# Load order, slot order, whole tail tiles, low parts on GpSimd: five small edits to a fused three-stage kernel

## The chip, the cores and the metric

The kernel runs on one core of a Trainium2 chip. The metric is the device time of one execution in microseconds, median over runs. One execution was also recorded by the hardware profiler; its times are from that one execution, and it has a time of its own.

TensorE multiplies matrices into PSUM, VectorE (DVE), ScalarE (ACT) and GpSimd (POOL) work element by element, and SyncE (SP) issues most of the transfers.

## The reference, cut to what matters

Three modules follow each other, for 8 batches of 576 tokens and 512 features (8 heads of 64).

```
# 1 retention
ret  = (q @ k.T / 8) * (gamma[h] ** (i - j) where i >= j else 0)   # B=8 H=8 S=576 D=64
x    = (ret @ v) with the heads side by side                       # [B, 576, 512]
# 2 attention by experts: 4 experts, the best 2 by gate
logits = x @ w_gate;  w = softmax of the best 2
for e in 4 experts:
    q, k, v = x @ wq[e], x @ wk[e], x @ wv[e]                      # 64 wide
    out += w[e] * (causal_softmax(q @ k.T / 8) @ v) @ wo[e]
# 3 mixing, with x = out
theta = x @ w_theta
y = w_tok_r @ (x * cos(theta)) + w_tok_i @ (x * sin(theta))        # over the tokens
u = x + y
return u + relu(u @ w_ch)
```

## The kernel before, in words

**Exact products.** An fp32 product is made of two rounded parts. `split` (L102) writes the high part with ACT and the low part, source minus high part, with VectorE. `mm3` (L97) is three matmuls: high by high, high by low and low by high. Nearly every matrix of stages 2 and 3 thus has a high and a low tile (`WH`, `WL`; `xh`, `xl`; `zh`, `zl`; `uh`, `ul`).

**Tiling.** The 576 tokens are five tiles of 128, 128, 128, 128 and 64 rows (`ROWS`). The tail, the tile of 64, is in places joined with the tail of the other batch of a pair: tile 4 of a pair g holds rows 0 to 63 of the first batch's tail and rows 64 to 127 of the second's.

**Stage 1** is a recurrence over the tiles. `ret_scores` (L136) makes the scores of a tile in two PSUM tiles called `w` and multiplies them by the decay; `ret_out` (L157 to L178) updates the state, makes the output in another `w` tile, and turns it into `xt`, `xh` and `xl`: VectorE (L175), ACT (L177), GpSimd (L178). `proj_qk` (L198 to L215) makes queries and keys of a half of the tokens (288 wide): twelve matmuls into one `w` tile, then its split. A key (`KN`) takes one ACT and one VectorE instruction, a query (`U`) two of each. `proj_v` (L229) makes the values and the gate's logits of one tile: four matmuls with the high part of x and of the weights, four with the low part of the weights, four with the low part of x.

**The weights** of the projections, `w1`, are 4 tiles of 128 x 772: columns 0 to 511 belong to queries and keys, 512 to 771 to values and gate. `load_w1` (L400) loads one tile whole, `split_w1` (L405) splits it. At the start (L486 to L502) the first batch's five retention steps, its value projections and its first query and key are written out by hand, with `work(-1, ...)` naming the projections.

**Stage 2** runs 80 slots (b, p, m), ten for each batch: scores of a query tile, softmax, transposes, products. Beside it each slot does what the table `SLOTS` (L43) names: projections ("Q01" the queries of expert pair 0 and token half 1, "K" keys, "v2" the values of tile 2, "g" the gate; small letters are of the next batch), and a retention step of the next batch (R0 to R5). `LAST` is the table of the last batch. The PSUM pool that holds `w` has three buffers (`WB`), used in turn by projections, scores of retention and its output. A job list turns the fp64 weights of stage 3 into high and low parts (`convert`, L421 to L441, mostly VectorE, ACT and GpSimd): 40 jobs for theta and token weights, due up to slot `JOBS[0]`, and 13 for the channel weights, due up to `JOBS[1]`.

**Stage 3**: `token_tile` makes x and theta of a tile, `z_tile` (L551) makes x cos and x sin and splits them (`zh`, `zl`; the tail's `zth`, `ztl`). `mix` (L656) adds in four PSUM accumulators the token products (L693), and x by a transpose on TensorE (`add_x`, L683), for one batch and one half of the features: 16 times. Then u is split, and `channel` (L706) multiplies it by the channel weights, GpSimd adding the low part at the end (L719). The gate's products for the outputs of stage 2 (`load_o`, L514) stand on GpSimd.

**What sets the order.** Up to the end of stage 2 TensorE runs its instructions in the order of the program. The other engines' order, and TensorE's in stage 3, is set by a scheduler when the kernel is built; each engine then runs its list in order.

## Time and profile before

| | |
|---|---|
| median of 3 runs | 955.18 us (954.91 to 955.77) |
| the profiled execution | 958.07 us, span 956.3 us |
| TensorE matmuls | 925.0 us, 97% of the span |
| TensorE weight loads | 854.3 us, 89% |
| VectorE | 643.0 us, 67% |
| ScalarE | 441.0 us, 46% |
| GpSimd | 247.8 us, 26% |

Busy times are sums over the span, and overlap. A busy share of 97% is a mean: stages with waits stand beside stages without. TensorE's granted clock is a share of full speed; at full speed it runs at 2.4 GHz, at half at 1.2 GHz. Stages 1 and 2 take the time up to about 514 us, with a passage to 541 us; the mixing takes the rest.

### The profile page before, as it was taken

The page shows a single profiled execution, that of the slowest core. Times are in us where ns is not written, and L with a number is a line of the kernel's source. Part 1 is how long each engine was busy: PE and PEld are TensorE (multiplying, and loading weights), DVE is VectorE, ACT ScalarE, POOL GpSimd, SP SyncE. Part 2 cuts the span into 40 slices and gives each one's busy share as a digit, 9 for nine tenths or more (in the row PEclk, how much of TensorE's full clock was granted, in tenths as well). Part 3 has the DMA queues.
Part 4 walks back from the last instruction along what each step waited for, and adds up shares of the span by engine and source line. Part 5 has one row for each costly group of instructions (what it writes and reads, how often), then busy time and mean ns, then how long its engine had stood idle before and what let it go on. Part 6 is the DMA issues. An engine that isn't in the chain of part 4 may idle for free.

```text
span 956.3 us, 21524 instructions
## 1 busy us (share of the span) xinstructions
PE 925.0 (97%) x8090; PEld 854.3 (89%) x8090; DVE 643.0 (67%) x1843; ACT 441.0 (46%) x1198; POOL 247.8 (26%) x290
## 2 busy tenths in 40 slices
PE   6989999999999999999999799999999999999998
PEld 5879989898998989988778799999999999999998
DVE  5377777867688787777669845684648755485623
ACT  2255555655565665555666414343234532344320
POOL 6315243452434434242312120111202101020100
PEclk9999999999999999999999899999999999999999
DMA  9757666576665666645784210111101001010001
GB/s 273 204 143 209 177 201 161 165 229 182 201 171 175 197 196 202 166 124 155 214 304 156 98 51 1 63 38 51 51 1 50 26 12 39 1 51 1 25 26 50
DMA packets 81016, 115.69 MB, mean 121 GB/s; under 512 B 17680, under 2 KB 55952, under 8 KB 80912
## 3 DMA queue, kind: packets, MB, share of 16 engines
q1 hardware_dynamic: 80768, 114.03, 40.1%
q8 instruction: 64, 1.05, 0.5%
q0 software_dynamic: 144, 0.28, 0.2%
q14 instruction: 40, 0.33, 0.1%
HBM read 71.94 MB, written 23.74 MB: 100 GB/s over the span
## 4 chain that ended last, share of the span: by engine, by line
PE 79%; DVE 9%; ACT 5%; DMA 3%; issue 2%; SPq 1%; POOL 1%; DVEq 0%; ACTq 0%; POOLq 0%
PE acc L693 24%; PE w L98 8%; PE w L99 8%; PE w L100 8%; PE w L229 6%; PE a L294 5%; PE w L136 5%; PE a L360 4%; PE a L341 3%; PE w L164 3%; PE w L168 3%; PE acc L683 2%; ACT P L302 2%; PE pS L157 1%; DVE U L215 1%
## 5 line engine op out<-in xcount | busy, mean ns | idle before, releaser
L693 PE MATMUL acc<-TK,zh 128*128 128x256 f32 (+1 forms) x1024 | 185.9, 304 | 3.7 <-DVE ul L104 2.4
L693 PEld LDWEIGHTS acc<-TK,zh 128*128 128x128 f32 x1024 | 154.1, 192 | 4.3 <-issue 2.6
L302 ACT ACTIVATE P<-P,st 128x128 f32<-128x128 f32 (+4 forms) x160 | 95.7, 599 | 76.1 <-DVE st L297 75.3
L693 PE MATMUL acc<-TK,zl 128*128 128x256 f32 (+1 forms) x512 | 111.1, 298 | 0.0
L719 POOL TENSOR_TENSOR o<-o,ul 128x576 f32<-128x576 f32 x28 | 42.4, 1519 | 222.3 <-DVE o L714 214.1
L693 PEld LDWEIGHTS acc<-TK,zl 128*128 128x128 f32 x512 | 87.1, 191 | 0.1
L561 ACT ACTIVATE cs<-cs 128x512 f32<-128x512 f32 x72 | 45.2, 630 | 90.7 <-DVE cs L559 85.0
L297 DVE CUSTOM_DVE_ANT_0 P<-a,cm 128x128 f32<-128x128 f32 (+4 forms) x160 | 72.1, 477 | 14.8 <-PE a L294 14.2
L98 PE MATMUL w<-uh,CH 128*128 128x256 f32 (+1 forms) x256 | 76.0, 298 | 3.3 <-ACT uh L103 2.6
L563 DVE SCALAR_TENSOR_TENSOR cs<-cs,x 128x512 f32<-128x512 f32 x72 | 62.0, 868 | 25.0 <-ACT cs L561 24.8
L294 PE MATMUL a<-KK,U 128*64 128x288 f32 (+4 forms) x384 | 76.8, 328 | 2.0 <-issue 0.9
L103 ACT ACTIVATE zh<-cs 128x512 fp32r<-128x512 f32 x64 | 40.3, 630 | 81.7 <-PE acc L693 65.3
L104 DVE TENSOR_TENSOR zl<-cs,zh 128x512 fp32r<-128x512 f32 x64 | 44.6, 699 | 48.9 <-ACT zh L103 48.1
L98 PE MATMUL w<-xh,WH 128*128 128x288 f32 x256 | 76.0, 297 | 0.0
L99 PE MATMUL w<-ul,CH 128*128 128x256 f32 (+1 forms) x256 | 75.7, 296 | 0.0
L100 PE MATMUL w<-uh,CH 128*128 128x256 f32 (+1 forms) x256 | 75.7, 296 | 0.0
L100 PE MATMUL w<-xh,WL 128*128 128x288 f32 x256 | 75.3, 294 | 0.0
L99 PE MATMUL w<-xl,WH 128*128 128x288 f32 x256 | 75.3, 294 | 0.0
L136 PE MATMUL w<-qz,kt 128*64 128x128 f32 (+1 forms) x576 | 57.5, 323 | 9.8 <-DVE U L215 7.3
L437 POOL TENSOR_TENSOR r<-r,ex 128x192 f32<-128x192 f32 (+1 forms) x51 | 29.5, 579 | 142.0 <-ACT hl L438 59.0
L104 DVE TENSOR_TENSOR ul<-acc,uh 128x256 fp32r<-128x256 f32 x64 | 25.8, 451 | 59.2 <-ACT uh L103 58.8
L294 PEld LDWEIGHTS a<-KK,U 128*128 128x128 f32 (+1 forms) x384 | 53.6, 171 | 12.6 <-issue 6.2
(141 smaller groups left out, 2265.9 us busy)
## 6 DMA issues: line engine op xcount, KB each, us to landing
kv<-kv SPq DMA_DIRECT2D x40, 512.0 KB
KK<-KN SPq DMA_DIRECT2D x128, 144.0 KB
raw<-wd SPq DMA_DIRECT2D x43, 192.0 KB
qz<-qk SPq DMA_DIRECT2D x64, 128.0 KB
kt<-qk SPq DMA_DIRECT2D x32, 256.0 KB
out<-o SPq DMA_DIRECT2D x28, 288.0 KB
td<-hl SPq DMA_DIRECT2D x27, 192.0 KB
TK<-td SPq DMA_DIRECT2D x9, 576.0 KB
```

The source lines that it names most:

```text
L98: nc.tensor.matmul(ps, ah, bh, start=first, stop=False)
L99: nc.tensor.matmul(ps, ah, bl, start=False, stop=False)
L100: nc.tensor.matmul(ps, al, bh, start=False, stop=last)
L104: nc.vector.tensor_sub(l, src, h)
L136: nc.tensor.matmul(ps[e][g, i, :, j * 64:R], t[:, hp, j * 64:j * 64 + 64], qz[:, :, hp, j * 64:R], start=True, stop=True, skip_group_check ...
L229: nc.tensor.matmul(ps[:R], x[:, kt, cs], W[:, kt, w0:w0 + NV], start=x is xh and W is WH and kt == 0, stop=x is xl and kt == 3)
L294: nc.tensor.matmul(ps[s][:R], U[:, s, rs], KK[:, s, x, j0:j1], start=x == 0, stop=x == 1)
L297: MARK["dve"] = nc.vector.tensor_tensor_reduce(Ps[s][:R, j0:j1], ps[s][:R], cm[:R, o + j0:o + j1], 1.0, st[:R, 0, s:s + 1] if i else 3.0e3 ...
L302: MARK["act"] = nc.scalar.activation(Ps[s][:R, :n], Ps[s][:R, :n], AF.Exp, bias=st[:R, last, s:s + 1], scale=-1.0, accum_out=SUM[p][:R, m, ...
L561: nc.scalar.activation(cs, cs, AF.Sin)
L563: nc.vector.scalar_tensor_tensor(z, cs, -1.0, x2[:, None, ds].to_broadcast([128, 2, 256]), op0=OP.mult, op1=OP.mult)
L693: nc.tensor.matmul(acc[d][j], A[:, dc], TK[:, kt, W, t0:t1], start=q == 0 and n == 0, stop=q == 8 and n == 2)
```

## The change

Five edits:

- The value and gate columns of the four `w1` tiles are loaded first and split first; the other columns are loaded after the inputs of retention step 2 and split after its output. The order of the hand-written start moves with it.
- In `SLOTS`, the queries of pair 1 come before its keys.
- In `add_x`, the tail is transposed as a whole 128 x 128 tile. For the second batch of a pair a matrix `swapped`, the identity with its halves exchanged, brings rows 64 to 127 to the front. What lands beyond column 64 is not read.
- For the first two batches (g is 0) the low part of tiles 1, 3, 5 and 7 is made by GpSimd: eight instructions.
- The conversions are due up to slots 56 and 71.

```diff
@@ -40,13 +40,13 @@
 PB_N = 5
-SLOTS = [("Q01 K10", "R0"), ("", ""), ("K11 Q10", ""), ("Q11", "R1"), ("", "R2"),
+SLOTS = [("Q01 Q10", "R0"), ("", ""), ("Q11 K10", ""), ("K11", "R1"), ("", "R2"),
          ("v0", "R3"), ("v1", ""), ("v2 k00", "R4"), ("q00", "R5"), ("v3 k01 v4 g", "")]
...
-JOBS = (58, 75)
+JOBS = (56, 71)
 EARLY = 9
@@ -78,6 +78,7 @@
     ident = consts.tile([128, 128], F32, name="ident")
+    swapped = consts.tile([128, 128], F32, name="swapped")
@@ -99,9 +100,9 @@
         nc.tensor.matmul(ps, ah, bl, start=False, stop=False)
         nc.tensor.matmul(ps, al, bh, start=False, stop=last)
-    def split(h, l, src):
+    def split(h, l, src, eng=None):
         nc.scalar.activation(h, src, AF.Copy)
-        nc.vector.tensor_sub(l, src, h)
+        (eng or nc.vector).tensor_sub(l, src, h)
     MARK = {}
@@ -397,22 +398,29 @@
     wst = []
-    def load_w1(kt):
-        st = w1s.tile([128, NW1], F32, name="wst", bufs=4)
-        nc.sync.dma_start(st, w1[kt * 128:(kt + 1) * 128, :])
-        wst.append(st)
-
-    def split_w1(kt):
-        split(WH[:, kt, :], WL[:, kt, :], wst[kt])
+
+    WP = [slice(512, NW1), slice(0, 512)]
+
+    def load_w1(kt, x):
+        if not x:
+            wst.append(w1s.tile([128, NW1], F32, name="wst", bufs=4))
+        nc.sync.dma_start(wst[kt][:, WP[x]], w1[kt * 128:(kt + 1) * 128, WP[x]])
+
+    def split_w1(kt, x):
+        split(WH[:, kt, WP[x]], WL[:, kt, WP[x]], wst[kt][:, WP[x]])
     for kt in range(4):
-        load_w1(kt)
+        load_w1(kt, 0)
     for c in range(2, LDB):
         loads(0, c)
+    for kt in range(4):
+        load_w1(kt, 1)
     with tc.issue_after(MARK["pool"].ins):
         nc.gpsimd.dma_start(cm, cst[:, o:o + 1088])
     nc.sync.dma_start(tie, cst[:, o + 1088:o + 1088 + E * E].rearrange("p (a b) -> p a b", a=E))
     nc.sync.dma_start(ident, cst[:, 0:128])
+    for s in range(2):
+        nc.gpsimd.tensor_copy(swapped[:, s * 64:s * 64 + 64], ident[:, 64 - s * 64:128 - s * 64])
     def convert(cvt, h, l, src, n):
@@ -489,17 +497,18 @@
     ret_out(0, 0)
     make_gt(1)
     for kt in range(4):
-        split_w1(kt)
-        if kt == 1:
-            ret_out(0, 1)
-    for c in range(2, NCH):
-        make_gt(c)
-    w1s.release()
+        split_w1(kt, 0)
+    ret_out(0, 1)
     work(-1, "v0 v1")
     for c in range(2, NCH):
         ret_scores(0, c)
+        make_gt(c)
         ret_out(0, c)
-        work(-1, ("", "v2 k00", "q00 v3 k01 v4 g")[c - 2])
+        if c == 2:
+            for kt in range(4):
+                split_w1(kt, 1)
+        work(-1, ("v2 k00", "q00 v3", "k01 v4 g")[c - 2])
+    w1s.release()
     X2, NR, OL = {}, {}, {}
@@ -564,7 +573,7 @@
         if i != 4:
             zh = zp.tile([128, 2, 256], F32R, name="zh", bufs=4)
             zl = zp.tile([128, 2, 256], F32R, name="zl", bufs=4)
-            split(zh, zl, z)
+            split(zh, zl, z, nc.gpsimd if g == 0 and i % 2 else None)
             ZT[g, i, h] = (zh, zl)
             return
         ZT[g, i, h] = []
@@ -656,8 +665,8 @@
     def mix(b, h):
         g, w = divmod(b, 2)
         tiles = [0, 1, 2, 3, 4] if w == 0 else [4, 5, 6, 7, 8]
-        acc = [[ps2.tile([128, t1 - t0], F32, name=f"acc{d}{i}", bufs=1, padded_shape=[128, 512])
-                for i, (t0, t1) in enumerate(TS)] for d in range(2)]
+        bank = [[ps2.tile([128, 512], F32, name=f"acc{d}{i}", bufs=1) for i in range(2)] for d in range(2)]
+        acc = [[bank[d][i][:, :t1 - t0] for i, (t0, t1) in enumerate(TS)] for d in range(2)]
         ks = []
         for i in tiles:
             if w == 0 or i != 4:
@@ -672,16 +681,14 @@
                 ks += [(m, zh[:, 0, :], zl[:, 0, :], i), (4 + m, zh[:, 1, :], zl[:, 1, :], None)]
         def add_x(i):
             x2 = X2[g, i]
-            if i == 4:
-                r, m = slice(w * 64, w * 64 + 64), 4
-            else:
-                r, m = slice(0, 128), i if i < 4 else i - 5
+
+            m = i % 5
             j = 0 if m < 2 else 1
             t0 = m * C - TS[j][0]
             for d in range(2):
                 dd = h * 256 + d * C
-                nc.tensor.matmul(acc[d][j][:, t0:t0 + ROWS[m]], x2[r, dd:dd + C], ident[r, r], start=False,
-                                 stop=False, is_transpose=True, skip_group_check=True)
+                nc.tensor.matmul(bank[d][j][:, t0:t0 + C], x2[:, dd:dd + C], swapped if i == 4 and w else ident,
+                                 start=False, stop=False, is_transpose=True, skip_group_check=True)
         for q, (kt, zh, zl, i) in enumerate(ks):
             if q and i is not None:
```

**How the lists move.** The rows below are the lists of instructions as built: line, operation, output and inputs, shape of the output; `x8` means eight in a row. Line numbers after the change are one to nine higher.

TensorE at the start, from retention step 2 on, before: the output of step 2 (`w` from `sm` and `vp`) is followed by the scores of the next step, and the value projection follows step 3.

```order
L157 MATMUL pS<-vp,kv 64x64 x8
L164 MATMUL w<-qz_126,S_122 64x128 x8
L168 MATMUL w<-sm_127,vp 64x128 x2
L168 MATMUL w<-sm_128,vp 64x128 x2
L136 MATMUL w<-qz_124,kt 64x256 x2
L136 MATMUL w<-qz_124,kt 64x2x64 x2
L157 MATMUL pS<-vp,kv 64x64 x8
L164 MATMUL w<-qz_124,S_123 64x128 x8
L229 MATMUL w<-WH,xh 128x260 x4
L229 MATMUL w<-WL,xh 128x260 x4
L229 MATMUL w<-WH,xl 128x260 x4
L98 MATMUL w<-xh,WH 128x288
```

The same place after:

```order
L137 MATMUL w<-qz_127,kt 64x256 x2
L137 MATMUL w<-qz_127,kt 64x2x64 x2
L158 MATMUL pS<-vp,kv 64x64 x8
L165 MATMUL w<-qz_127,S_123 64x128 x8
L169 MATMUL w<-sm_128,vp 64x128 x2
L169 MATMUL w<-sm_129,vp 64x128 x2
L230 MATMUL w<-WH,xh 128x260 x4
L230 MATMUL w<-WL,xh 128x260 x4
L230 MATMUL w<-WH,xl 128x260 x4
L99 MATMUL w<-xh,WH 128x288
L100 MATMUL w<-xl,WH 128x288
L101 MATMUL w<-xh,WL 128x288
```

The value projection of tile 2 now stands directly behind the output of step 2, with the first key's matmuls (L99 to L101) behind it.

VectorE around slots 2 and 3 of a batch, before: `U` is a query's split, `P,st` the softmax row statistics, `PT` copies of transposes, `ex` and `b` parts of a conversion, and `xt` the output of a retention step.

```order
L433 SCALAR_TENSOR_TENSOR b_2696<-ex,b_2696 128x192
L346 COPY PT<-a 128x2x128
L215 SCALAR_TENSOR_TENSOR U<-w,U 64x288 x2
L434 TENSOR_SCALAR ex<-b_2696 128x192
L297 ISA P,st<-a,cm 128x512
L297 ISA st 128x1
L346 COPY PT<-a 128x2x128
L348 COPY PT<-a 128x128
L215 SCALAR_TENSOR_TENSOR U<-w,U 64x288 x2
L175 TENSOR_TENSOR xt<-w,gt 128x512
```

After, in the same slots:

```order
L216 SCALAR_TENSOR_TENSOR U<-w,U 64x288 x2
L347 COPY PT<-a 128x2x128
L105 TENSOR_TENSOR KN<-w,KN 128x288
L298 ISA P,st<-a,cm 128x512
L298 ISA st 128x1
L436 TENSOR_SCALAR b_2831<-raw 128x192
L441 SCALAR_TENSOR_TENSOR b_2831<-ex,b_2831 128x192
L347 COPY PT<-a 128x2x128
L105 TENSOR_TENSOR KN<-w,KN 128x288
L349 COPY PT<-a 128x128
L442 TENSOR_SCALAR ex<-b_2831 128x192
L176 TENSOR_TENSOR xt<-w,gt 128x512
```

Slot 2 has a query's and a key's split, and slot 3 a single instruction for a key (`KN`) where there were two for a query; a conversion stands between.

GpSimd from the last conversions to the first channel products, before: `hl` is a conversion, `ol` the gate's products, `o` the additions at the end of `channel`.

```order
L441 TENSOR_TENSOR hl<-d,r 128x128
L514 TENSOR_TENSOR ol<-ol,og 128x1152 x3
L719 TENSOR_TENSOR o<-o,ul 128x576 x4
L514 TENSOR_TENSOR ol<-ol,og 128x1152
L719 TENSOR_TENSOR o<-o,ul 128x576 x4
```

After:

```order
L449 TENSOR_TENSOR hl<-d,r 128x128
L523 TENSOR_TENSOR ol<-ol,og 128x1152 x3
L105 TENSOR_TENSOR zl<-cs,zh 128x512
L523 TENSOR_TENSOR ol<-ol,og 128x1152
L105 TENSOR_TENSOR zl<-cs,zh 128x512 x2
L523 TENSOR_TENSOR ol<-ol,og 128x1152
L105 TENSOR_TENSOR zl<-cs,zh 128x512 x3
L726 TENSOR_TENSOR o<-o,ul 128x576 x4
L105 TENSOR_TENSOR zl<-cs,zh 128x512 x2
```

The eight low parts (`zl`) stand among the products and the additions: one between the third and the fourth product, two between the fourth and the fifth, three before the first additions and two behind them.

## Rows read from the trace of the kernel before

**Rows 1.** stretches of the span: start:end, length, busy us of each engine (instructions), granted clock, DMA share, GB/s

```profile
core 0: us, PE busy (x) PEld busy (x) DVE busy (x) ACT busy (x) POOL busy (x), PEclk, DMA share, GB/s
15.20:19.90 4.70, 1.83 (x8) 0.98 (x6) 4.70 (x7) 3.08 (x5) 4.49 (x2) 0.93 1.07 270
19.90:26.00 6.10, 4.68 (x20) 4.15 (x22) 3.13 (x3) 0.46 (x3) 4.55 (x4) 0.50 1.07 271
448.00:514.40 66.40, 62.17 (x389) 49.20 (x387) 50.05 (x156) 44.98 (x123) 13.12 (x12) 1.00 0.68 213
514.40:530.20 15.80, 15.77 (x118) 15.55 (x118) 15.21 (x35) 8.49 (x15) 2.98 (x1) 1.00 0.81 283
530.20:541.20 11.00, 5.98 (x26) 5.43 (x25) 10.57 (x25) 5.44 (x13) 2.86 (x1) 0.70 0.24 74
541.20:957.00 415.80, 410.36 (x2840) 392.70 (x2839) 242.53 (x536) 140.89 (x283) 50.77 (x31) 1.00 0.09 31
```

**Rows 2.** waits of TensorE: instruction <- what ended it, us, times, longest

```profile
PE w L136 <- DVE U L215: 7.3, 8, 1.6
PE w L229 <- DVE WL L104: 2.7, 2, 1.4
PE w L98 <- ACT uh L103: 2.6, 1, 2.6
...
PE acc L693 <- DVE ul L104: 2.4, 1, 2.4
```

**Rows 3.** timeline of TensorE: start, us, instruction; whole pair of transposes

```profile
524.50 0.43 PE L693 MATMUL acc<-TK,zl 128*128 128x256 f32 x2
524.77 0.38 PE L683 MATMUL acc<-ident,x 128*128 128x128 f32 x2
524.90 0.78 PE L693 MATMUL acc<-TK,zh 128*128 128x256 f32 x4
```

**Rows 4.** timeline of TensorE, a tail's pair of 64 rows

```profile
527.92 0.42 PE L693 MATMUL acc<-TK,zl 128*128 128x256 f32 x2
528.27 0.33 PE L683 MATMUL acc<-ident,x 64*128 64x64 f32 x2
528.54 0.81 PE L693 MATMUL acc<-TK,zth 128*128 128x256 f32 x4
```

**Rows 5.** timeline of TensorE, slot 3 of batches 1 and 2; waits in brackets

```profile
121.01 1.27 PE L136 MATMUL w<-qz,kt 128*64 128x256 f32 x12 [0.41 <-DVE U L215]
...
178.83 1.27 PE L136 MATMUL w<-qz,kt 128*64 128x256 f32 x12 [1.61 <-DVE U L215]
```

**Rows 6.** timeline of ACT and VectorE, slot 3 of batch 2

```profile
176.92 0.80 ACT L212 ACTIVATE U<-w 64x288 fp32r<-64x288 f32 x2
...
177.76 0.93 DVE L215 SCALAR_TENSOR_TENSOR U<-w,U 64x288 fp32r<-64x288 f32 x2 [1.15 <-ACT U L212]
```

**Rows 7.** a key's split: duration ns min/median/max, first and last start, forms

```profile
L103 ACT ACTIVATE KN<-w x32: 387/410/412, 37.0 to 456.5; 128x288 fp32r<-128x288 f32 x32
L104 DVE TENSOR_TENSOR KN<-w,KN x32: 445/457/460, 37.4 to 457.0; 128x288 fp32r<-128x288 f32 x32
```

**Rows 8.** timeline of the start, second tile: GpSimd and TensorE

```profile
19.29 1.74 POOL L178 TENSOR_TENSOR xl<-xt,xh 128x512 fp32r<-128x512 f32 x1 [0.21 <-ACT xh L177]
...
24.89 1.07 PE L229 MATMUL w<-WH,xl 128*128 128x260 f32 x4
```

**Rows 9.** timeline of the start, retention step 2: last matmuls and low part

```profile
28.77 1.21 PE L168 MATMUL w<-sm,vp 128*64 128x128 f32 x16
...
31.52 1.28 POOL L178 TENSOR_TENSOR xl<-xt,xh 128x512 fp32r<-128x512 f32 x1 [5.68 <-ACT xh L177]
```

**Rows 10.** timeline of the start, step 4 (64 rows), low part

```profile
40.38 0.74 POOL L178 TENSOR_TENSOR xl<-xt,xh 128x256 fp32r<-128x256 f32 x1 [2.77 <-ACT xh L177]
```

**Rows 11.** low parts of rotated tiles on VectorE: duration ns min/median/max

```profile
L104 DVE TENSOR_TENSOR zl<-cs,zh x64: 674/692/1065, 511.9 to 923.6; 128x512 fp32r<-128x512 f32 x64
```

**Rows 12.** timeline of the first pair of mixing: GpSimd and VectorE

```profile
521.27 2.98 POOL L514 TENSOR_TENSOR ol<-ol,og 128x1152 f32<-128x1152 f32 x1 [12.33 <-DMA og<-gd]
...
521.60 4.28 DVE L104 TENSOR_TENSOR ztl<-cs,zth 64x256 fp32r<-64x256 f32 x4
```

## What is predicted

> **What bounds the kernel now.** I read first the table of engine busy times, then the view that sums each engine's busy time by stretch, then TensorE's waits by releaser, and only then single instructions at the places the change touches. The stretches [rows 1] show that TensorE sets the end: it is busy 410.36 of the 415.80 us of the mixing phase, while VectorE has 242.53 and GpSimd 50.77 us there. Three stretches are different: 15.20 to 26.00 at the start (TensorE waits, and its granted clock is 0.93 and then 0.50 of full speed), the slots up to 514.40 (62.17 busy of 66.40), and the passage into the mixing phase at 530.20 to 541.20 (5.98 busy of 11.00, granted clock 0.70). The waits [rows 2] are few: 7.3 us of retention scores (L136) that wait for VectorE's split of a query projection, 2.7 us of value projections that wait for the low half of the weights, and 2.6 and 2.4 us in the passage, for the split of u. So an edit pays in full where it takes an instruction off TensorE or ends one of these waits; elsewhere it pays nothing, but it can make a new wait.
>
> **1. Tails as whole tiles.** Each of the 16 pairs (batch, half of the features) adds x through transposes. Between the start of the low-part matmuls in front and the start of those behind, a pair of 128-row transposes takes 524.90 − 524.50 = 0.40 us [rows 3] and a 64-row pair takes 528.54 − 527.92 = 0.62 [rows 4]: 0.22 more, for a quarter of the output. The change makes all the short ones (two to a pair) long: 16 × 0.22 = 3.5 us off a bound engine, −3.5. The matrix `swapped` costs two small copies on GpSimd at the start, which I cost at nothing: they queue behind the identity's load and nothing reads them for 500 us. If the long form with another matrix were no shorter it is 0; the rows show no reason.
>
> **2. Queries ahead of keys.** In slot 3 the step R1 of the next batch's retention takes its score tiles from the same three PSUM buffers as the projection before it, so the second score tile waits until that projection is split out. For a query the split is ACT 0.80 (two) and VectorE 0.93 (two), one behind the other: 176.92 to 178.69, and the scores go on at 178.83 after 1.61 us of waiting [rows 5, 6]. A key needs one ACT instruction of 0.41 and one VectorE instruction of 0.46 [rows 7]: 0.87 instead of 1.73, so 0.86 sooner. R1 comes in batches 0 to 6. Its seven waits make 6.3 of the 7.3 us: four short ones, as the 0.41 at 121.01, that sum to 1.7, and three of 1.4 to 1.6, as that at 178.83 [rows 5]; the eighth (0.95) stands in the first slot, behind the gate's chain, and stays. The four short ones go (−1.7). Of the three long ones each loses 0.86, and since slot 2 now ends in a key's split too, VectorE is free up to 0.46 sooner; I take half of that, as a conversion may fill the gap: 3 × 1.09 = 3.3. Sum −5.0; the bounds are −1.7 (a key's split that queues behind the exponentials on ACT and comes no sooner in the three) and −6.3. Slot 0 gets a second query split instead of a key's, 0.86 later; its retention step has only scores there, the buffer of the second projection is not taken again until the next step, so I cost it at nothing; without that cover it is as much as 0.86 in each of seven batches, which takes the sum to its upper bound or a little over.
>
> **3. Value weights first.** Now the value projection of the second tile ends at 24.89 + 1.07 = 25.96 [rows 8]. With its weights first the 2.7 us of waiting for them go, and what holds it is the low part of the retention output, xl, which GpSimd finishes at 19.29 + 1.74 = 21.03. Then only eight matmuls are left, four for each of two tiles, 1.07 a four at that clock: 23.2, so −2.8. Against that, the work that used to stand between a retention step and the projection that reads it moves away. For step 2 TensorE's last retention matmul ends at 28.77 + 1.21 = 29.98, and xl on GpSimd at 31.52 + 1.28 = 32.80 [rows 9]: a chain of 2.82 through VectorE, ACT and GpSimd. "v2" now follows directly; its eight matmuls on the high part take about 1.07 (eight at the full clock as long as four at half), so it waits 1.75. "v3" has "q00" ahead and waits about 0.2. "k01" follows step 4 directly; its GpSimd part is 0.74 instead of 1.28 [rows 10], so the chain is about 2.82 × 0.74 / 1.28 = 1.6, and its second matmul reads xl: 1.5. New waits 3.5, sum +0.7. Bounds: −6.6, if the two early stretches (10.80 us) shrink to their work of 1.83 + 4.68 × 0.5 = 4.2 us [rows 1] and no new wait arises; +3.5, if nothing is won at the second tile. I take +0.7, the sum of the rows' own chains. Queues passed: SP issues four more loads ahead of the work, and the first retention inputs of step 2 stand behind 260 of 772 columns instead of all of them; the other columns' split stands behind step 2's output, where VectorE and ACT have just the chain above.
>
> **4. Low parts on GpSimd.** Eight instructions leave VectorE, where each takes 0.69 [rows 11], for GpSimd, where xl of the same 128 × 512 elements takes 1.28 [rows 9]. Four of them belong to the first pair of the first batch, where VectorE is busy 15.21 of 15.80 us and TensorE 15.77; the other four follow in the passage. For the good side: 4 × 0.69 = 2.8 us of VectorE ahead of the split of u, which TensorE waits for afterwards. Against: VectorE and GpSimd stop each other. While GpSimd multiplied for 2.98 us from 521.27, four VectorE pieces of 64 × 256 took 4.28 [rows 12]; four whole low parts would be 2.8. GpSimd also has these products in its own queue, and the order places one between the low parts of tile 1 and tile 3, so tile 3 can be late for TensorE.
>
> The Trainium skill (SBUF — State Buffer, "Who interferes with whom") says that VectorE and GpSimd share a port pair as an exclusive lock, held for a whole instruction, when VectorE reads two operands from SBUF. The 4.28 us in the row agree. By that rule each low part on GpSimd would hold VectorE for 1.28 and save it 0.69, so four would cost +2.4 instead of −2.8.
>
> From the rows alone a low part costs VectorE between −0.69 (nothing stopped) and +0.6 (1.28 of stopping less 0.69). Over four: −2.8 to +2.4, and up to +4 if the passage's 0.70 clock lasts that much longer. I take +1.5, nearer the stopped end, which the row of 4.28 shows.
>
> **5. Conversions.** The second group (channel weights) moves some slots forward from the last ones before 514.40. TensorE's idle time in 448.00 to 514.40 is 66.40 − 62.17 = 4.2 us [rows 1]. An eighth of it is my estimate, −0.5; the same instructions may do as much harm in the busier slots where they go. Bounds −1 and +1.
>
> **Sum.** −3.5 − 5.0 + 0.7 + 1.5 − 0.5 = −6.8. The profiled execution took 958.07 us (span 956.3 and 1.8 around it), so 951.3 on that scale. The median of the runs is 955.18, lower by 2.89: I predict 948.4.
>
> **Rivals.**
> - (a) Start and low parts both pay: GpSimd's low parts run beside VectorE and the early stretches shrink to their work. −3.5 − 6.3 − 6.6 − 2.8 − 0.5 = −19.7, so 935.5. For it: idle time is there to be taken in both places. Against: xl on GpSimd still ends the start's chains, and [rows 12].
> - (b) The waits only move: the key's split queues on ACT behind the exponentials (−1.7), the start's new waits eat its gain (+3.5), the low parts cost +1.5 and the tails give −3.5. −0.2, so 955.0. For it: three of the seven waits are already much longer than the split's own difference. Against: in [rows 6] VectorE waits 1.15 for ACT, so ACT's length counts directly.
> - (c) Slower: TensorE's clock falls in the first pair of the mixing phase. The low part of tile 3 waits on GpSimd behind a product (2.98) and TensorE stands still before it; in the passage that follows, two waits of about 2.5 us go with a granted clock of 0.70. If three quarters of the 15.8 us at 514.40 to 530.20 run at the 1.2 GHz level, they cost 0.75 × 15.8 = 12 more. −3.5 − 5.0 + 0.7 + 12 − 0.5 = +3.7, so 958.9. It decides once TensorE stands still for about 2 us before tile 3. Against: by the order the low part of tile 1 and three products are done before tile 3's is wanted, and there is some slack.
>
> **Chances.** Forecast 0.73, (a) 0.08, (b) 0.11, (c) 0.08. A measurement of this kernel can tell about 0.2% (1.9 us) from no change. Forecast and (a) are faster: 0.81; (b) is the same: 0.11; (c) slower: 0.08. The range goes from 942 (terms 3 and 4 each some 3 us better than taken) to 955.2 (term 2 at its upper bound and term 4 at +4 give 954.2, and most of (b) lies below 955.2); it leaves out (a), (c) and a quarter of (b).
>
> **What would show it.** Tails: 160 transposes of one shape, and 0.40 at each tail. Order: L136's wait on U gone but for the first slot's, and a smaller one on KN. Start: TensorE's wait for the low weights gone; waits for xl of about 1.7 and 1.5 us before "v2" and "k01". Low parts: instructions of 1.3 us on GpSimd, and VectorE instructions beside them stretched by as much; granted clock 1.00 in the first pair. I am wrong if the passage gets longer than 14 us, if the start's new waits exceed 5 us in sum, or if slot 0 shows the wait that slot 3 lost.

## The result, and the profile after

The changed kernel took 965.07 us (median of 8 runs, 962.99 to 966.38), the kernel before, in the runs beside it and earlier ones, 956.8 us: a ratio of 1.0077, 95% interval 1.0059 to 1.0096. The medians differ by 8.3 us, the ratio by 7.4 us: slower, where 6.8 us faster was forecast. The profiled execution of the changed kernel has a span of 963.1 us, before 956.3.

Four points of the two traces cut this difference into stretches: the first score matmul of stage 2, the first matmul of the mixing, the first of its third pair (batch, half), and its last.

| us | before | after | difference | forecast |
|---|---|---|---|---|
| start, to the first score of stage 2 | 45.4 | 50.1 | +4.7 | +0.7 |
| slots, to the first mixing matmul | 469.0 | 471.1 | +2.1 | −5.5 |
| first two pairs and the passage | 52.4 | 55.9 | +3.5 | +1.1 (+1.5, tails −0.4) |
| the other 14 pairs | 372.4 | 369.2 | −3.2 | −3.1 |

The tails did what was forecast; every other stretch is longer than forecast. The stretches of the trace after (columns as in [rows 1]):

```profile
24.60:36.00 11.40, 9.75 (x95) 8.27 (x96) 3.11 (x7) 2.83 (x8) 4.32 (x4) 0.83 0.51 155
...
521.20:536.90 15.70, 15.70 (x118) 15.50 (x118) 13.31 (x29) 7.00 (x14) 5.65 (x3) 1.00 0.62 203
536.90:547.30 10.40, 1.47 (x5) 1.06 (x4) 7.75 (x15) 5.13 (x11) 5.10 (x3) 0.67 0.21 57
```

The first pair of the mixing (521.20 to 536.90) ran without a wait at full clock, so rival (c) did not happen. The 10.40 us behind it hold 1.47 us of TensorE's work, where 11.00 us of before hold 5.98. From the end of the first pair to the first matmul of the second it is 10.4 us, before 5.9. TensorE's waits after:

```profile
PE w L99 <- ACT uh L104: 8.9, 1, 8.9
PE w L137 <- DVE KN L105: 4.2, 5, 1.7
...
PE w L230 <- ACT xh L178: 2.5, 2, 1.5
PE w L230 <- DVE WL L105: 1.4, 2, 0.8
```

Against [rows 2]: one wait for u of 8.9 instead of two of 2.6 and 2.4; the wait of the scores for a query's split (7.3) is now one for a key's split (4.2, five times); the value projections wait less for their weights (1.4 instead of 2.7) but now for `xh`.

**The tails.** All transposes have one form, and the pair at a tail takes 535.09 − 534.68 = 0.41 us between the low parts around it, against 0.62 in [rows 4]:

```profile
534.68 0.43 PE L700 MATMUL acc<-TK,zl 128*128 128x256 f32 x2
534.95 0.38 PE L690 MATMUL acc<-ident,x 128*128 128x128 f32 x2
535.09 0.78 PE L700 MATMUL acc<-TK,zth 128*128 128x256 f32 x4
```

**Slot 3 of batch 2.** What was forecast is there: the key's split is done at 182.28, ahead of the scores at 182.88, which wait for nothing (against [rows 5, 6]).

```profile
181.40 0.39 ACT L104 ACTIVATE KN<-w 128x288 fp32r<-128x288 f32 x1
181.82 0.46 DVE L105 TENSOR_TENSOR KN<-w,KN 128x288 fp32r<-128x288 f32 x1
...
182.88 1.47 PE L137 MATMUL w<-qz,kt 128*64 128x256 f32 x16
```

From slot to slot the changed kernel wins up to 2.2 us at slots 4 and 5 of a batch (nothing in batch 1). But it loses 2.3, 0.7, 2.5 and 4.6 us between slots 7 and 8 of batches 0 to 3. Slot 7 of batch 0, after (SPq is SyncE's queue of transfers, `raw` a conversion's input, `tt` and `hl` its output, `gd` the gate's values):

```profile
68.75 0.59 POOL L449 TENSOR_TENSOR hl<-d,r 128x192 fp32r<-128x192 f32 x1
...
75.75 3.12 SPq L317 DMA_DIRECT2D gd<-nwt  x4
...
79.73 0.57 SPq L456 DMA_DIRECT2D tt<-hl  x1
...
83.30 0.58 SPq L429 DMA_DIRECT2D raw<-wd  x1
...
86.22 0.45 SPq L429 DMA_DIRECT2D raw<-wd  x1
90.78 0.56 SPq L456 DMA_DIRECT2D tt<-hl  x1
91.45 2.50 SPq L429 DMA_DIRECT2D raw<-wd  x2
...
92.86 0.26 DVE L436 TENSOR_SCALAR b<-raw 128x192 int32<-128x192 int32 x1 [2.52 <-DMA raw<-wd]
...
94.68 0.46 DVE L105 TENSOR_TENSOR KN<-w,KN 128x288 fp32r<-128x288 f32 x1
...
95.19 0.54 PE L137 MATMUL w<-qz,kt 128*64 128x128 f32 x5 [1.46 <-DVE KN L105]
```

And before:

```profile
65.32 0.33 SPq L421 DMA_DIRECT2D raw<-wd  x1
...
80.54 0.42 SPq L421 DMA_DIRECT2D raw<-wd  x1
...
84.34 0.33 SPq L421 DMA_DIRECT2D raw<-wd  x1
...
85.93 0.26 DVE L428 TENSOR_SCALAR b<-raw 128x192 int32<-128x192 int32 x1
...
86.53 0.58 SPq L448 DMA_DIRECT2D tt<-hl  x1
...
88.12 0.46 DVE L104 TENSOR_TENSOR KN<-w,KN 128x288 fp32r<-128x288 f32 x1 [0.20 <-ACT KN L103]
...
89.67 0.61 PE L136 MATMUL w<-qz,kt 128*64 128x128 f32 x8
```

Each trace has 51 loads and 51 conversions in the same order, so they can be counted through. The conversion at 92.86 reads the load issued at 86.22, 6.64 us earlier; the loads from 91.45 on, which stand behind a store that waits until 90.78 for its result, belong to later conversions, and the next one does not wait. VectorE reaches the conversion at 90.34, stands still for 2.52 us before it, and the key's split (k00) stands behind it in VectorE's list. Before, this same load (the fourth) was issued at 80.54, its conversion began at 85.93 without a wait, and the load ahead of it (the third) was issued at 65.32 instead of 83.30.

After, SyncE's list has these two loads behind the gate's stores, the inputs of retention steps and the stores of earlier conversions, which it issues without a pause from 75.75 to 86.67. The store at 79.73 does not wait for its conversion: GpSimd ended `hl` at 69.34. In all eight places where VectorE waits, the load was issued 3.6 to 6.6 us ahead of its conversion, and the store ahead of it had had its result for 5 to 12 us. The largest single loss, 4.6 us in batch 3, is of the same kind: VectorE waits 2.61 us for `raw`, the softmax statistics stand behind it, and TensorE waits 2.8 us for those.

Over the whole trace VectorE waits for `raw` 3.6 us in 3 places before and 19.2 us in 8 after:

```profile
DVE b L436: 19.2, 8
```

**The passage after.** The split of u stands on ACT behind the rotated tiles that follow, and these behind GpSimd:

```profile
537.57 1.26 POOL L105 TENSOR_TENSOR zl<-cs,zh 128x512 fp32r<-128x512 f32 x1 [7.88 <-issue]
538.79 2.61 POOL L523 TENSOR_TENSOR ol<-ol,og 128x1152 f32<-128x1152 f32 x1
538.86 2.68 DVE L567 TENSOR_SCALAR cs<-nr 128x256 int32<-128x256 int32 x1 [1.54 <-POOL zl L105]
...
545.43 1.29 ACT L104 ACTIVATE uh<-acc 128x256 fp32r<-128x256 f32 x4
545.85 1.44 PE L99 MATMUL w<-uh,CH 128*128 128x256 f32 x4 [8.92 <-ACT uh L104]
```

VectorE waits 1.54 us to overwrite the tile `cs` whose low part GpSimd is still making, then runs an operation of 0.29 us for 2.68 beside the product on GpSimd; u is split 8.5 us after the accumulators were full.

**The start after.** The last retention matmul of step 2 ends at 27.62 + 1.21 = 28.83:

```profile
27.62 1.21 PE L169 MATMUL w<-sm,vp 128*64 128x128 f32 x16
30.34 0.75 PE L230 MATMUL w<-WH,xh 128*128 128x260 f32 x4 [1.51 <-ACT xh L178]
30.92 0.64 PE L230 MATMUL w<-WL,xh 128*128 128x260 f32 x4
31.70 1.15 PE L230 MATMUL w<-WH,xl 128*128 128x260 f32 x4
```

"v2" waits 1.51 for the high part and about 0.3 for the low part, 1.8 in sum, where the forecast had 1.75 (as one wait for the low part). Behind it, the granted clock of the stretch 24.60 to 36.00 is 0.83, where the forecast counted with the full clock. The key "k01" waits 1.0 for the high part and 0.4 for the low part, 1.4 in sum (forecast 1.5).

### The profile page after: what moved, and what is told of

Its sections match the earlier page's. It is cut to its first block, busy times and chain, and to the rows that moved or that the text cites. A ratio compares the mean times of both kernels' runs of the same rounds, so it can differ in the third digit from the quotient of the medians.

```text
span 963.1 us, 21546 instructions
## 1 busy us (share of the span) xinstructions
PE 924.6 (96%) x8090; PEld 855.9 (89%) x8090; DVE 636.0 (66%) x1839; ACT 440.4 (46%) x1202; POOL 255.4 (27%) x300
## 4 chain that ended last, share of the span: by engine, by line
PE 56%; DVE 4%; DMA 3%; issue 2%; ACT 2%; POOL 1%; SPq 1%; POOLq 0%; ACTq 0%; DVEq 0%
PE acc L700 23%; PE w L99 7%; PE w L100 7%; PE w L101 6%; PE a L295 2%; PE a L361 2%; PE w L230 2%; PE acc L690 2%; PE a L342 2%; PE w L137 2%; PE w L169 1%; DMA TK<-td 1%; PE w L165 1%; PE pS L158 1%; DVE cs L572 1%
## 5 line engine op out<-in xcount | busy, mean ns | idle before, releaser
L570 ACT ACTIVATE cs<-cs 128x512 f32<-128x512 f32 x72 | 45.3, 630 | 93.8 <-DVE cs L568 91.1
L99 PE MATMUL w<-uh,CH 128*128 128x256 f32 (+1 forms) x256 | 76.2, 300 | 10.0 <-ACT uh L104 8.9
L298 DVE CUSTOM_DVE_ANT_0 P<-a,cm 128x128 f32<-128x128 f32 (+4 forms) x160 | 71.8, 477 | 14.2 <-PE a L295 13.8
L99 PE MATMUL w<-xh,WH 128*128 128x288 f32 x256 | 77.0, 301 | 1.0 <-ACT xh L178 1.0
L101 PE MATMUL w<-xh,WL 128*128 128x288 f32 x256 | 76.1, 297 | 0.0
L101 PE MATMUL w<-uh,CH 128*128 128x256 f32 (+1 forms) x256 | 75.7, 296 | 0.0
L105 DVE TENSOR_TENSOR zl<-cs,zh 128x512 fp32r<-128x512 f32 x56 | 39.2, 700 | 38.7 <-ACT zh L104 37.8
L123 POOL TENSOR_TENSOR vp<-kv,gam 128x512 f32<-128x512 f32 x40 | 42.6, 1067 | 74.5 <-DMA kv<-kv 43.2
```

The source lines that it names most:

```text
L99: nc.tensor.matmul(ps, ah, bh, start=first, stop=False)
L101: nc.tensor.matmul(ps, al, bh, start=False, stop=last)
L105: (eng or nc.vector).tensor_sub(l, src, h)
L123: MARK["pool"] = nc.gpsimd.tensor_mul(vp, u[:, 1, :].rearrange("p (h d) -> p h d", h=H), gam[:, c, :, None].to_broadcast([128, H, D]))
L298: MARK["dve"] = nc.vector.tensor_tensor_reduce(Ps[s][:R, j0:j1], ps[s][:R], cm[:R, o + j0:o + j1], 1.0, st[:R, 0, s:s + 1] if i else 3.0e3 ...
L570: nc.scalar.activation(cs, cs, AF.Sin)
```

## The experiments

The theory after reading the two traces: three losses, in the start, in the conversions that block VectorE's list, and in the passage. What was open is which edit makes which. The lengths of the stretches in all profiled executions (us; "last 14" are the pairs 3 to 16) and the ratio of the timed runs to the kernel before with its interval:

| run | start | slots | first two pairs, passage | last 14 | ratio |
|---|---|---|---|---|---|
| before | 45.4 | 469.0 | 52.4 | 372.4 | 1 |
| after | 50.1 | 471.1 | 55.9 | 369.2 | 1.0077 [1.0059, 1.0096] |
| e1_old_due | 45.9 | 472.3 | 56.4 | 368.9 | 1.0058 [1.0039, 1.0078] |
| e2_zl_vector | 48.0 | 472.4 | 51.5 | 368.9 | 1.0027 [1.0009, 1.0045] |
| e3_old_start | 45.2 | 474.6 | 55.1 | 368.9 | 1.0080 [1.0055, 1.0106] |
| e4_tails_slots | 46.9 | 470.7 | 48.8 | 369.3 | 0.9953 [0.9936, 0.9970] |
| e5_slots_prefetch | 47.3 | 464.4 | 48.5 | 368.8 | 0.9909 [0.9882, 0.9935] |
| e6_before_prefetch | 46.9 | 469.6 | 52.1 | 372.5 | 0.9978 [0.9957, 1.0000] |
| e7_zl_gpsimd | 44.5 | 472.0 | 56.2 | 368.9 | 1.0035 [1.0016, 1.0055] |
| e8_zl_gpsimd_3cs | 45.6 | 470.9 | 56.5 | 368.9 | 1.0048 [1.0029, 1.0068] |
| e9_prod_vector | 47.7 | 467.5 | 46.0 | 367.6 | 0.9856 [0.9830, 0.9882] |
| e10_prod_vector_zl_gpsimd | 45.8 | 464.7 | 50.2 | 367.6 | 0.9897 [0.9872, 0.9923] |
| e11_zl_gpsimd_g1 | 45.0 | 465.0 | 49.1 | 369.1 | 0.9922 [0.9894, 0.9949] |
| e12_prefetch_early_due | 47.1 | 464.4 | 51.5 | 369.2 | 0.9909 [0.9883, 0.9935] |
| e13_new_start | 50.5 | 463.3 | 46.0 | 367.6 | 0.9880 [0.9858, 0.9902] |
| e14_old_slots | 45.3 | 467.5 | 46.0 | 367.6 | 0.9890 [0.9871, 0.9910] |

**e1_old_due**, the changed kernel with the old due slots:

```diff
-JOBS = (56, 71)
+JOBS = (58, 75)
```

> The changed kernel with the old due slots (58, 75) for the conversions; all else as changed. Theory A (the earlier conversions stand in VectorE's and ACT's lists ahead of a key's split while their raw weights have not landed): VectorE's wait for the raw weights falls from 19.2 us back to about 4, the retention scores' waits for the key's split (4.2 us) go, the slots lose no time to before, and the kernel is about 10 us shorter than the changed one, at a ratio to before of about 0.997. Rival B (the waits come from the new slot table, which moves the keys' transfers in SyncE's list): the waits for raw weights and for the key's split stay, and the time stays within 2 us of the changed kernel's.

Theory A fell. The slots took 472.3 us, no less than after, and the scores still waited for a key's split:

```profile
PE w L137 <- DVE KN L105: 4.8, 5, 1.9
```

So the blocked list isn't made by the due slots. The ratio, 1.0058 against 1.0077, can't be told from the changed kernel's.

**e2_zl_vector**, the changed kernel with the low parts on VectorE:

```diff
-            split(zh, zl, z, nc.gpsimd if g == 0 and i % 2 else None)
+            split(zh, zl, z)
```

> The changed kernel with all low parts of rotated tiles on VectorE again. Theory A (GpSimd's low parts keep the tile buffer of the rotation and lock VectorE, which delays the split of u in the passage): TensorE's wait for u at the first channel products goes from 8.9 us to about 5 in sum, and the kernel is 3.5 us shorter than the changed one. Rival B (the passage is longer because the gate's products on GpSimd come at another moment, as the second stage ends at another time): the passage stays, and the time within 1 us of the changed kernel's.

Theory A held: the passage fell by 4.4 us in the trace, and the ratio by 0.0050, 4.8 us. The wait for u was 5.6 in one piece.

**e3_old_start**, the changed kernel with the loads and the hand-written start of the kernel before (both hunks about `w1` undone).

> The changed kernel with the start as before (whole weight tiles loaded, old order of the first projections). Theory A (the start loses 4.7 us by the value and key projections that now stand directly behind the retention outputs they read, and by the low clock after these waits): the first scores of the second stage start at about 45.4 us instead of 50.1, and the kernel is 4.7 us shorter. Rival B (part of the 4.7 us, the 1.6 lost by 15 us with a granted clock of 0.66 before any changed work, belongs to the single execution): only about 3 us are won.

The start was back at 45.2 us, but the timed runs gained nothing (1.0080 against 1.0077): in this execution the slots took 474.6. Neither theory's number was met; the start's cost stayed open.

**e4_tails_slots**, tails and slot table alone (the edits of e1, e2 and e3 together).

> Only the whole tail tiles and the new slot table, the three other edits undone. Theory A (the losses are of the other three edits, the two kept edits give what the rows of before say): tails 3.5 us and slots 5 us shorter, so a ratio to before of about 0.991. Rival B (the slot table moves the waits rather than ends them): tails alone, a ratio of about 0.9965, with waits for a key's split in other slots that sum to some 5 us.

It lies between, and rival B names the place: the slots took 470.7 us, 1.7 more than before, with the new table alone. Up to slot 5 of batch 0 they won 1.6 us, and at slots 8 and 9 of that batch lost 3.9. VectorE waited for `raw` as in the changed kernel:

```profile
DVE b L432: 23.5, 9
```

So the slot table itself brings the late loads: with it, the list that the scheduler makes for SyncE has them later.

**e5_slots_prefetch**, as e4, with the raw weights loaded one job ahead, so that SyncE's list has the load earlier:

```diff
+            fetch(k)
+            fetch(k + 1)
...
-            convert(pl, t[:, 0, :], t[:, 1, :], wd[:, off + o:off + o + n], n)
+            convert(pl, t[:, 0, :], t[:, 1, :], RAWS[k], n)
```

> Tails and new slot table (the run e4_tails_slots), and each conversion's raw weights loaded one job earlier, so that in SyncE's list the load stands ahead of the store of the conversion before. Theory A (with the new slot table the load stands behind that store, the conversion waits for it in VectorE's and ACT's lists, and the key's split of slot 7 stands behind the conversion): VectorE's wait for raw weights falls from 23.5 us to under 6, the 9.8 us that the slots lose at slots 8 and 9 of batches 0 to 3 go, and the kernel is 7 to 10 us shorter than e4_tails_slots, at a ratio to before of about 0.987. Rival B (the conversions wait because the transfers themselves are slow among others, whatever the list's order): the waits stay and the time is within 1.5 us of e4_tails_slots.

Theory A held for the waits, and for about half of the time. SyncE's list ahead of slot 7 of batch 0, where the third and the fourth load now stand at 76.32 and 80.80 (80.01 and 82.93 in e4) and their conversions no longer wait:

```profile
76.32 0.55 SPq L424 DMA_DIRECT2D raw<-wd  x1
76.98 0.57 SPq L455 DMA_DIRECT2D tt<-hl  x1
...
80.80 0.54 SPq L424 DMA_DIRECT2D raw<-wd  x1
```

VectorE's wait for `raw` fell from 23.5 to 5.5 us, TensorE's for the key's split from 3.3 to 1.3:

```profile
DVE b L435: 5.5, 4
...
PE w L230 <- POOL xl L179: 2.9, 2, 1.7
```

The slots took 464.4 us, 6.3 less than in e4; the ratio fell by 0.0044 (4.2 us; 7 to 10 were expected). So late loads are shown as the cause, but not theory A's reason for their lateness, the store that waits for the conversion before: at the places of the waits no store did. Of the 9.8 us lost at slots 8 and 9, some 3.5 were still lost, in batches 2 and 3. There TensorE waits at "v2" for the low part of x, 1.73 and 1.22 us, as it does in e4 (2.8 in sum): in batch 2 GpSimd reaches it behind a product that waits 1.88 us for its own load (`kv`). This part is not the wait for raw weights, and the forecast of 7 to 10 had counted it in.

**e6_before_prefetch**, the kernel before with that load alone.

> The kernel before with the raw weights loaded one job earlier, nothing else. Theory A: before has little to win, since VectorE waits only 3.6 us for raw weights there and TensorE none of it; ratio within 0.998 to 1.001. Rival B (the earlier load is a gain by itself, not through the slot table's order): 5 us or more shorter, as in e5_slots_prefetch.

0.9978, at the edge of theory A's range, and slots 469.6. The early load gives little without the new table.

**e7_zl_gpsimd**, e4 with the eight low parts on GpSimd again.

> Tails and new slot table (as e4_tails_slots), and the eight low parts on GpSimd. Theory A (the low parts cost what the passage lost in the changed kernel): the passage's wait for u grows from 2.8 to 7 or more, and the kernel is 4 to 6.5 us longer than e4_tails_slots. Rival B (they cost little, and the passage's length goes by when the second stage ends): within 1.5 us.

Theory A: the passage grew from 48.8 to 56.2 us and the ratio by 0.0082 (7.9 us, above the forecast of 4 to 6.5). The waits for u came back:

```profile
PE w L99 <- ACT uh L104: 6.4, 1, 6.4
...
PE acc L695 <- DVE ul L105: 2.6, 1, 2.6
```

**e8_zl_gpsimd_3cs**, e7 with a third buffer for the rotated tile:

```diff
-        cs = zp.tile([128, 2, 256], F32, name="cs", bufs=2)
+        cs = zp.tile([128, 2, 256], F32, name="cs", bufs=3)
```

> As e7_zl_gpsimd, with three buffers instead of two for the rotated tile that the low part reads. Theory A (VectorE waits to overwrite the tile that GpSimd still reads): the wait of VectorE for GpSimd's low part goes, and at least half of the loss of e7_zl_gpsimd to e4_tails_slots is won back. Rival B (the lock between GpSimd and VectorE, with the products beside it, makes the loss): the loss stays, VectorE instructions of 2.6 us beside GpSimd's remain.

Theory A's gain did not come: 56.5 us, as long as e7. But its condition wasn't met either: VectorE still waited 1.18 us for GpSimd's low part in the passage (1.55 in e7), so the run does not tell the buffer from the lock. The product's shadow was there, as rival B says:

```profile
532.72 0.30 DVE L562 TENSOR_SCALAR cs<-nr 128x256 int32<-128x256 int32 x1 [1.18 <-POOL zl L105]
...
538.55 2.81 POOL L518 TENSOR_TENSOR ol<-ol,og 128x1152 f32<-128x1152 f32 x1
538.91 2.60 DVE L562 TENSOR_SCALAR cs<-nr 128x256 int32<-128x256 int32 x1
```

**e9_prod_vector**, e5 with the gate's products on VectorE:

```diff
-        nc.gpsimd.tensor_mul(OL[b], OL[b], gw)
+        nc.vector.tensor_mul(OL[b], OL[b], gw)
```

> As e5_slots_prefetch, with the gate's products of the second stage's outputs on VectorE instead of GpSimd (low parts on VectorE). Theory A (the products on GpSimd stop VectorE for their 2.8 us, in the passage too): VectorE instructions of 2.6 us or more go, a product on VectorE takes about 1.4 us, and the time is within 1.5 us of e5_slots_prefetch, as the passage's wait of 2.8 us is for ACT. Rival B (VectorE's list gets longer by the products just where it bounds): 2 us or more longer.

Better than either theory: 944.31 us (940.82 to 947.65), the fastest kernel of this study. A product takes 1.35 us on VectorE:

```profile
510.86 1.35 DVE L531 TENSOR_TENSOR ol<-ol,og 128x1152 f32<-128x1152 f32 x1
```

No VectorE instruction is stretched beside it, and the wait for u at the passage fell to 0.9 and 0.3 us; the passage took 46.0 us. Where the products stand, the traces give 2.5 us (passage) and 1.2 us (last 14 pairs) against e5; the slots of this one execution are 3.1 us longer than e5's.

**e10_prod_vector_zl_gpsimd**, e9 with the low parts on GpSimd.

> As e9_prod_vector, and the eight low parts of the first two batches on GpSimd. Theory A (the low parts' loss comes from the products that share GpSimd and stop VectorE): without products there the low parts cost less than 2 us against e9_prod_vector. Rival B (the loss is the chain through GpSimd itself: a low part takes 1.26 instead of 0.69, keeps the rotated tile, and the lists of ACT and VectorE put more of the next tiles ahead of u's split): 4 us or more longer than e9_prod_vector, with a wait for u of 6 us or more.

Between the two, nearer to rival B: the passage grew by 4.2 us (46.0 to 50.2), the ratio by 0.0041 (3.9 us; the intervals just overlap), with no product on GpSimd. The wait for u was 3.4, less than rival B named. So of e7's 7.4 us in the passage about 4 belong to the low parts themselves, and some 3 came with the products beside them.

**e11_zl_gpsimd_g1**, e5 with the low parts on GpSimd for the second pair of batches, `g == 1` instead of `g == 0`.

> As e5_slots_prefetch, with the low parts of tiles 1, 3, 5, 7 on GpSimd for the second pair of batches (g is 1) instead of the first: the same eight instructions, away from the passage. Both theories of the low parts' loss place it in the passage: within 1 us of e5_slots_prefetch. If a low part on GpSimd costs wherever it stands: 4 us or more longer.

0.9922 against 0.9909, and 369.1 against 368.8 us in the last 14 pairs, where these eight instructions stand: no cost that can be told. The place makes the price.

**e12_prefetch_early_due**, e5 with `JOBS = (56, 71)`.

> As e5_slots_prefetch, with the due slots (56, 71). Theory A (the due slots are of no weight once the loads stand early): within 1.5 us of e5_slots_prefetch. Rival B (the earlier conversions crowd the slots): 2 us or more longer.

The timed runs agree with theory A: 0.9909, the same as e5, though each interval is 2.5 us wide on either side. The trace doesn't: the slots are the same (464.4), but the passage is 3.0 us longer, and TensorE's wait for u is 5.7 us instead of 2.8:

```profile
PE w L99 <- ACT uh L104: 5.7, 1, 5.7
...
525.37 3.75 DVE L580 SCALAR_TENSOR_TENSOR cs<-cs,x 128x512 f32<-128x512 f32 x2
525.63 2.94 POOL L531 TENSOR_TENSOR ol<-ol,og 128x1152 f32<-128x1152 f32 x1 [5.32 <-DMA og<-gd]
```

The gate's product starts on GpSimd 14.2 us after the first mixing matmul, and the pair of VectorE instructions ahead of u's split takes 3.75 us beside it (1.30 in e5, where the product starts 18.8 us after that matmul, just behind the start of u's split). e2 and e4, which differ in the start as well, show the same: due slots (56, 71) with a product at 14.2 us and a passage of 51.5, and (58, 75) with one at 18.4 and 48.8.

**e13_new_start** and **e14_old_slots**: e9 with the new start, and e9 with the old slot table.

> As e9_prod_vector, with the new start (value weights first, projections directly behind the retention outputs). Theory A (the start's own cost is the +0.7 us of the prediction's rows, and the rest of the 4.7 us in the changed kernel's trace is the scatter of the start between executions, which was up to 3 us with one code): within 2 us of e9_prod_vector. Rival B (the start loses what the trace showed): 4 us or more longer.

> As e9_prod_vector, with the old slot table. Theory A (the new table gives the 5 us that the rows of before said once the raw weights are loaded early): 4 to 7 us longer than e9_prod_vector, with the seven waits of retention scores for a query's split back (about 7 us). Rival B (the table gives no net gain, and the early loads and the products on VectorE made all of it): within 1.5 us.

e13: 0.9880 against 0.9856, 2.3 us, intervals that overlap: nearer to theory A, and rival B's 4 us or more is not seen. e14: 0.9890, 3.3 us longer than e9, between the theories, again with intervals that overlap; the waits of the old table are back, as theory A says:

```profile
PE w L137 <- DVE U L216: 7.0, 8, 1.6
```

## Why the prediction was wrong, point by point

**1. Tails: right.** −3.2 us over 14 pairs, 0.23 a pair (forecast 0.22). It shows in every run that has the edit: 367.6 to 369.3 us for the last 14 pairs, against 372.4 and 372.5.

**2. Queries ahead of keys: the mechanism was right, the sum was wrong, and this is the largest failed step.** The waits at slot 3 went as forecast, and in e4 the slots 4 and 5 won 8.2 us over the seven batches, more than the upper bound of 6.3. The step that failed is the sentence that a conversion "may fill the gap". It counted the conversion's VectorE time, not its input. The new table also moved the conversions' loads in SyncE's list, to places behind other transfers, where they come too late. The instructions for `raw` then wait at the head of VectorE's and ACT's lists, and the next key's split or the softmax statistics behind them. What slot 3 gave, slot 7 took: 19.2 us of such waits instead of 3.6. A second, smaller cost stands at "v2", where TensorE waits for the low part of x (2.8 us in e4, 2.9 in e5, no such wait before). Rival (b), the waits only move, had the right kind, but placed it at slot 3 on ACT. With the loads ahead, the slots were 463.3 to 465.0 us in five of six runs with the new table (467.5 in the sixth, e9), and 469.6 and 467.5 in the two with the old one (e6, e14); before had 469.0. So the traces give mostly two to six us, none between e9 and e14, and the timed runs of these two 3.3: what the step had forecast, or somewhat less.

**3. Value weights first: undersized.** The second tile's value projection was won as forecast: it ended at 24.73 instead of 25.96, although in this execution the retention steps ahead ended 1.6 us later. The new waits were of the forecast size as well (1.8 at "v2", 1.4 at "k01"). The step that failed is that the sum counted the work around these waits at the full clock; the clock was 0.83 in 24.60 to 36.00. Over all runs the start took 45.9 to 50.5 us with the new order (four executions, mean 48.6) and 44.5 to 47.7 with the old one (twelve, mean 46.1): +2.5, not +0.7. Part of the 4.7 of the one trace belongs to the execution: its clock between 10 and 15 us, ahead of all changed work, was 0.66. Executions with that clock there took 46.9 to 47.7 us with the old order and 50.1 and 50.5 with the new, 3.1 more; those with 1.00 there took 44.5 to 45.8 and 45.9 and 48.0, 1.7 more. The 45.9 is e1, where the clock was 1.00 all along and the cost is about the forecast's. The timed runs give 2.3 us (e13) and nothing (e3), so the size stays open.

**4. Low parts on GpSimd: undersized, and past the bound.** Forecast +1.5, at most +4; two pairs of timed runs give 4.8 (after against e2) and 7.9 us (e7 against e4). The prediction had priced four instructions of the first pair by how much they stop VectorE. Only two stand there, the low parts of tiles 1 and 3; the count of four was wrong. The first pair didn't feel them: 15.70 us, TensorE busy throughout. The price fell in the passage, on those that follow, by the chain low part, buffer, next rotated tile, ACT's list, u; the sum had no term for that chain. It has one row that could have been read beforehand: the wait for u of 2.6 us in [rows 2] said that u's split stands behind the next tiles' work. The case of e11 shows that the same instructions have no cost that can be told where TensorE is busy nearly throughout. The Trainium skill (SBUF — State Buffer, "Who interferes with whom") warned with its lock, and the rows agree: 0.29 us became 2.68 beside a product of 2.61. That instruction reads a single operand, though, and the prediction had named the lock for two. The lock with the low parts explains only a part, since e10, without products, still lost 3.9 us. Which share of that is the longer chain and which the order of ACT's list is not settled. The two prices, 4.8 and 7.9, differ because e2 is itself slow in the passage: there, as in e12, the product on GpSimd stands in u's chain already (51.5 against e4's 48.8).

**5. Conversions: nothing in the timed runs (e12), forecast −0.5, but in the traces about +3 us in the passage.** The sum looked for the effect in the slots, which stayed the same. What moved is the moment of a product on GpSimd at the passage (e12 against e5, e2 against e4). With the low parts on GpSimd no such difference is seen (55.9 after, 56.4 in e1). The timed runs neither show these 3 us nor exclude them.

None of the prediction's three signs of being wrong came: the stretch of the passage is 10.40 us, the start's new waits sum to about 4 us, and slot 0 waits 0.6 us. The losses stand where no sign was set.

In the end +4.7 + 2.1 + 3.5 − 3.2 = +7.1 us by the stretches, against a difference of 6.8 us in the spans; behind the last mixing matmul the changed kernel is 0.3 us shorter.

## What to carry to other kernels

Before a step is costed that changes the order of work, follow its transfers in the issuing queue as well: a load that slips behind other transfers comes late, and an instruction that waits for it stops all that is behind it on its engine. Count loads and the instructions that read them through before one is put down to the other. Loads issued one round ahead in the program took most of these waits away here (23.5 to 5.5 us). Work moved to a slower engine is priced where the next thing waits for it, not where the engine it leaves is busiest; here eight instructions had no cost that could be told in one place and 4 to 8 us in another.

## What the runs showed that was not expected

A product of two SBUF operands of 128 x 1152 takes 1.35 us on VectorE (2.28 once, beside a low part on GpSimd in e10) and 2.61 to 3.20 on GpSimd (4.27 and 4.45 once each in e2 and e12), and on GpSimd it stretched VectorE's instructions from 0.29 to 2.6 us and more. Eight of them moved to VectorE made the kernel faster by 0.53% (e9 against e5, intervals that just touch), although VectorE was already the busier of the two.

The start of one and the same code differs by up to 3.2 us between executions with the old order and 4.6 with the new one, and the granted clock between 10 and 15 us is either about 0.66 or 1.00. A single trace can't tell an edit of 2 us there; executions with the same clock in that stretch can be compared more closely.
